# The channel loop of an attention and state-space training step: shared strips for the lag products, parameters for two blocks at once, basis rows in 2 KB pieces, states laid out by step

## The chip, the cores and the metric

The kernel runs on one core of a Trainium2 chip. The metric is the time of one execution on the device in microseconds (us), as the median of several runs; the time before is 2,733.29 us (three runs, 2,728.04 to 2,741.99). The profile is that of one further execution.

## The reference

A forward pass and all its gradients. The input x (2,048 tokens by 576 channels) goes through 32-head attention (`a`) and through a state-space convolution (`b`), and a gate mixes the two. The part that the change touches is `b` and its gradient:

```
logdA = dt * A                                   # A, B, C: 576 channels x 128 states, complex
P = exp(logdA[:, :, None] * l[None, None, :])    # l = 0 .. 2047
K = einsum("dn,dnl,dn->dl", C, P, dt * B).real   # one kernel of 2048 taps per channel
y = causal convolution of x with K, per channel (by FFT), + u * Dskip
out = g * a + (1 - g) * y
```

Returned are `out` and the gradients with respect to x, the attention's weights, A, B, C, log_dt, Dskip and the gate's weights. The kernel does the convolution without an FFT, in 16 time blocks of 128 tokens: within a block by a 128 x 128 Toeplitz matrix made of the first 128 taps, across blocks by 128 complex states per channel that step from block to block.

## The kernel before

There are three long stages: projections and attention with its gradients (to about 2,050 us), the channel loop (about 2,137 to 2,565 us, with a run-up before it), and a closing stage with the output projections. The order of the instructions on each engine is written out by hand; each engine, and SP and POOL as queues that issue transfers, takes its own in that order.

Beside attention, POOL computes the basis: for each channel the powers of its state factors, 128 states by real and imaginary part by 128 offsets, and stores it in DRAM as `E_d`, four channels (2 KB per partition) at a time (line 555).

The channel loop (lines 1481 to 1565) runs over 18 blocks of 32 channels. Iteration i finishes block i, steps the states of i+1, and prepares i+2 (`sb`) and i+3 (`mb`). What matters here, in the order of an iteration:

- `scan_open` and `scan` (704 to 733): DVE steps the states `HG` of blocks i and i+1 through 15 time blocks, two chains taken alternately, three instructions per step and chain. The factors come from `par`. `HG` has its four parts (real and imaginary, forward and backward in time) outermost and the step next.
- `rw1`, `rw2` (744 to 755): DVE weights the states with `par` and packs them as `Rw` for PE.
- `m_sum`, `m_fin` (637 to 648): PE sums the sheared lag products `skw` of block i+2 into the gradient of the first 128 taps.
- `m_part` (611 to 622), twice for block i+3, 16 channels each: for a channel one matmul of 128 x 32 weights (`gyp`: 16 columns of the incoming gradient, 16 of zeros) with 128 columns of `xs`, into its own 32 rows of a PSUM tile. The lower 16 rows get zeros. ACT copies the tile to `mst`; SP stores it in DRAM as `Md_d`, 32 rows of 144 floats per channel.
- `m_load` (604): POOL loads the next `xs` (1 MB, 8 KB per partition) and `gyp`. `m_skw` (629): SP reads `Md_d` back with a row pitch one element shorter than the rows, which turns diagonals into columns; the 16 columns of zeros that end each row of `mst` fill the corners.
- `sums` (847) and `load_par` (668) on POOL; `turn_e` (655): PE transposes the basis `E1n` of block i+2 and ACT copies it out as `E1e`; `k0` and `k0_out` (761, 772): PE makes the first 128 taps of block i+1, ACT copies them, SP stores them in `Kp_d`.
- `uv` (688): PE projects x and the gradient onto the basis, ACT copies to `UV`. `t0` (778): PE applies the Toeplitz matrix `T0w`; `t0_load` (853): SP loads the next `T0w` from `Kp_d` with overlapping rows (1 MB, 8 KB per partition), one buffer.
- `ybp` (787): PE adds what the states give (`Rw` with `E1n`), and when a half of `E1n` is used up, `load_en` (678) has POOL load half of block i+3 into its place (1 MB, 8 KB per partition).
- `yd_out`, `pairs1`, `pairs2`, `psum` (797 to 839): results out, and products of the two state chains, which PE sums.

So SP's order in an iteration is: two stores of `Md_d`, four sheared loads `skw`, the store of `Kp_d`, the load of `T0w`. POOL's is: `xs`, `gyp`, two additions, three loads of `par`, the two halves of `E1n`, and in turn `RXn` or `yd_d`. In the run-up (1447 to 1480, and 1270 to 1279 beside the end of attention) SP issues all loads.

Of the kernel before, what the change touches and what calls it, by code (L numbers as in the profile page):

```python
# [17 lines left out]
P = 128  # L18


def build(tc, aps, dbg_aps=None, stages=("s1", "attn", "post", "s4", "final")):
# [40 lines left out]
    with ExitStack() as gctx:  # L62
# [33 lines left out]
        E_d = dram.tile([P, D, 2, P], BF, name="E_d")  # L96
# [7 lines left out]
        Md_d = dram.tile([D, 2 * SUB, MW], F32, name="Md_d")  # L104
# [382 lines left out]
        def basis_ops(pool, k0, k1):  # L487
# [41 lines left out]
            def e_main(k, c):  # L529

                q = k * CE + c
                nl = (NA - 1) * NBT

                def first():
                    Eo[q] = pool.tile([P, EH, 2, P], BF, tag="Eo", bufs=2, name="Eo")
                    pl(Eo[q][:, :, :, 0:NBT], T_[:, :, c:c + EH, 0:NBT].rearrange("p r c b -> p c r b"),
                       sgn.unsqueeze(1).unsqueeze(3).to_broadcast([P, EH, 2, NBT]), A.mult)
                eops.append((0.45, first))
                for ri in range(2):
                    st = []  # L540
# [63 lines left out]
        def m_load(b, dma=nc.gpsimd.dma_start):  # L604
            xs = xss[b] = Q["pl"].tile([P, NSUB, SUB, CB], BF, tag="xs", bufs=1, name="xs")
            src = bass.AP(tensor=xb_d.tensor, offset=xb_d[b:b + 1, 0:1, 0:1].offset,
                          ap=[[XR * SUB * CB, NB], [SUB * CB, NSUB], [1, NSUB * SUB * CB]])
            dma(xs.rearrange("p e t c -> p (e t c)"), src)
            dma(Q["gyp2"][b % 2][:, 0:SUB, :].rearrange("p t c -> p (t c)"), gyb_d[b])

        def m_part(b, u):
            d0 = b * CB
            gyp, xs = Q["gyp2"][b % 2], xss[b]
# [8 lines left out]
            Q["mdma"](Md_d[d0 + u * 16:d0 + (u + 1) * 16].rearrange("(q g) t w -> (g t) q w", g=4), mst)  # L622
# [6 lines left out]
        def m_skw(b):  # L629
            skw = skws[b] = Q["pl"].tile([P, CB // 8, P], F32, tag="skw", name="skw")  # L630
            for v in range(CB // 8):
                dd = b * CB + v * 8
                src = bass.AP(tensor=Md_d.tensor, offset=Md_d[dd:dd + 1, 0:1, SUB - 1:SUB].offset,
                              ap=[[2 * SUB * MW, 8], [MW - 1, SUB], [1, P]])
                Q["mdma"](skw[:, v, :], src)
# [31 lines left out]

        def load_par(b, dma=nc.gpsimd.dma_start):
            if b == NBLK - 1:
                par = Q["pw"].tile([P, XB, NCOL], BF, tag="RX", bufs=2, name="par_l").bitcast(F32)[:, 0:12, :]  # L670
            else:
# [32 lines left out]
        def scan_open(b):  # L704
            B_ = blk(b)
            HG = B_["HG"] = Q["pw"].tile([P, 4, NS, CB], F32, tag="HG", bufs=2, name="HG")
            UVk = B_["UVk"] = B_["UV"][:, :, 0:2 * NB, :].rearrange("p r (s k) c -> p r s k c", s=2)
            nc.vector.tensor_copy(HG[:, :, 0, :].rearrange("p (r s) c -> p r s c", s=2), UVk[:, :, :, 0, :])

        def scan(*chains):  # L710

            def part(b, s_):
                B_ = blk(b)
                HG, ZZ = B_["HG"], B_["par"][:, 0:8, :].rearrange("p (m q) c -> p m q c", m=2)
                if s_ is None:
                    return HG, ZZ, B_["UVk"], 4
                return HG[:, s_::2], ZZ[:, :, s_::2], B_["UVk"][:, :, s_:s_ + 1], 2

# [3 lines left out]
            for t in range(max(k1 - k0 for _, _, k0, k1 in todo_)):  # L722
                live = [(x, p_, k0 + t) for x, p_, k0, k1 in todo_ if k0 + t < k1]
                tz = {}
                for x, (HG, ZZ, UVk, n), k in live:
                    tz[x] = Q["pw"].tile([P, 2, 4, CB], F32, tag=f"tz{x}", bufs=2, name="tz")[:, :, 0:n]
                    nc.vector.tensor_tensor(tz[x], HG[:, :, k - 1, :].unsqueeze(1).to_broadcast([P, 2, n, CB]), ZZ, op=A.mult)
                for x, (HG, ZZ, UVk, n), k in live:
                    t0v = tz[x][:, 0].rearrange("p (r s) c -> p r s c", r=2)
                    nc.vector.tensor_tensor(t0v, t0v, UVk[:, :, :, k, :], op=A.add)  # L730
                for x, (HG, ZZ, UVk, n), k in live:
                    t0v, t1v = [tz[x][:, m].rearrange("p (r s) c -> p r s c", r=2) for m in range(2)]
                    nc.vector.tensor_tensor(HG[:, :, k, :].rearrange("p (r s) c -> p r s c", r=2), t0v, t1v[:, ::-1], op=A.add)

        def cast1(b, nm, s_):
            B_ = blk(b)
            HGv = B_["HG"].rearrange("p (r s) k c -> p r s k c", s=2)
            B_[nm] = Q["pw"].tile([P, 2, NS, CB], BF, tag=nm, name=nm)
            nc.scalar.copy(B_[nm], HGv[:, :, s_, ::-1, :])
# [4 lines left out]
        def rw1(b):  # L744
            B_ = blk(b)
            for nm, r_, tg in (("wa", 8, "wA"), ("wb", 9, "wB")):
                B_[nm] = Q["pw"].tile([P, 4 * NS, CB], F32, tag=tg, name=nm)
                nc.vector.tensor_tensor(B_[nm], B_["HG"].rearrange("p q k c -> p (q k) c"),  # L748
                                        B_["par"][:, r_, :].unsqueeze(1).to_broadcast([P, 4 * NS, CB]), op=A.mult)
# [7 lines left out]
        def wk_cast(b):  # L757
            wk = blk(b)["wk"] = Q["pw"].tile([P, 2, CB], BF, tag="wk", bufs=2, name="wk")
            nc.scalar.copy(wk, blk(b)["par"][:, 10:12, :])
# [101 lines left out]
        def open_loads():  # L861
# [3 lines left out]
            Q["gyp2"], Q["mst2"] = [], []  # L865
# [4 lines left out]
            for u in range(2):  # L870
                m_u = Q["pl"].tile([P, 4, MW], F32, tag=f"mst{u}", name=f"mst{u}")
                nc.gpsimd.memset(m_u[:, :, P:MW], 0.0)
                Q["mst2"].append(m_u)
# [20 lines left out]
        def load_xtok():  # L894
            x_v = x2.rearrange("(t p) d -> p t d", p=P)
            for nm, shape, dt_, n in (("xs", [P, NSUB, SUB, CB], BF, 7), ("RXn", [P, 2 * NB, XB], BF, 3), ("gyp0", [P, 2 * SUB, CB], BF, 1),
                                      ("gyp1", [P, 2 * SUB, CB], BF, 1), ("mst0", [P, 4, MW], F32, 2), ("mst1", [P, 4, MW], F32, 2)):
# [49 lines left out]
        if "attn" in stages:  # L947
# [5 lines left out]
            with ExitStack() as ctx:  # L953
# [316 lines left out]
                for x, f in ((15, lambda: pt_close("a", open_loads)), (15, lambda: m_load(0, nc.sync.dma_start)), (17, lambda: load_rx(0, nc.sync.dma_start)),  # L1270
                             (21, lambda: m_part(0, 0)), (22, lambda: m_part(0, 1)), (23, lambda: pt_close("b", lambda: open_en(0))),
# [138 lines left out]
        if "s4" in stages:  # L1410
# [8 lines left out]
            with ExitStack() as ctx:  # L1419
# [27 lines left out]
                with tc.manual_schedule(engines={mybir.EngineType.SP}):  # L1447
# [13 lines left out]
                    m_part(1, 0)  # L1461
                    m_part(1, 1)
# [11 lines left out]
                    m_part(2, 0)  # L1474
                    m_part(2, 1)
# [5 lines left out]
                    for i in range(NBLK):  # L1481
# [38 lines left out]
                        if sb == NBLK - 1:  # L1520
                            load_par(sb)
# [303 lines left out]
```

## Time and profile before

| | |
|---|---|
| median of three runs | 2,733.29 us |
| the profiled execution | 2,736.89 us |
| its span, first to last instruction | 2,734.8 us |
| PE busy | 2,414.4 us (88%) |
| ACT busy | 2,356.0 us (86%) |
| DVE busy | 2,301.4 us (84%) |
| POOL busy | 1,803.1 us (66%) |
| mean granted clock of PE | 0.962 |
| moved by DMA | 492.20 MB in 1,169,461 packets |

The busy times are averages over stages of different kinds: in the attention stage ACT is busy all the time, in the channel loop PE, DVE and the DMA engines are all near full, and in the closing stage PE is. A row of the profile names the line, the engine, the operation and its tiles; "SPq" and "POOL ... DMA_DIRECT2D" are issues of transfers, whose own time is only that of the issue. Idle time stands in brackets with the work that ended it. Some transfers of the loop, with the median time from issue to landing, which the profile gives for those that POOL issues:

| transfer | count, size | us to landing |
|---|---|---|
| `E1n` from `E_d` (POOL) | 30 of 1,024 KB | 6.6 |
| `xs` from `xb_d` (POOL) | 14 of 1,024 KB | 12.1 |
| `par` from `par_d` (POOL) | 45 of 64 KB | 7.6 |
| `T0w` from `Kp_d` (SP) | 18 of 1,024 KB | not given |
| `Md_d` from `mst` (SP) | 36 of 288 KB | not given |
| `skw` from `Md_d` (SP) | 72 of 64 KB | not given |

### The profile page before, as it was taken

The numbers are of one execution on the slowest core, as the hardware profiler recorded it, in microseconds if no ns is written. First come the engines' busy times: TensorE is split into PE (matmuls) and PEld (weight loads), VectorE is DVE, ScalarE is ACT, GpSimd is POOL, SyncE is SP. The second block draws the span as 40 slices with busy tenths as digits, with TensorE's granted clock in tenths as the row PEclk, the third lists the DMA queues.
The fourth block names the chain that finished last, engine by engine and source line by source line (L and its number), as shares of the span: only waits on it lengthen the run. The fifth ranks groups of instructions, "written<-read, shape, count | busy, mean of one in ns | idle before, by whom it ended". The sixth has DMA issues, their size and how long they took to land. (4 is left out here: it accounts for less than half of the span.)

```text
span 2734.8 us, 70124 instructions
## 1 busy us (share of the span) xinstructions
PE 2414.4 (88%) x27411; PEld 1148.3 (42%) x27411; DVE 2301.4 (84%) x4142; ACT 2356.0 (86%) x2744; POOL 1803.1 (66%) x2856
## 2 busy tenths in 40 slices
PE   8798989999888988988998898998986789898889
PEld 4433333333333333333333333333323688888656
DVE  4749999999899999999999999998975798889864
ACT  5489999999999999999999999999974789788211
POOL 0179888888888888798888878888601244335321
PEclk9989999999999999999999999999977899999989
DMA  7637799879879978977988898797779799887894
GB/s 226 186 97 164 149 170 177 159 163 178 169 154 175 177 151 169 185 155 163 171 167 158 160 179 161 157 177 153 147 134 223 195 251 249 235 251 236 236 266 126
DMA packets 1169461, 492.20 MB, mean 180 GB/s; under 512 B 1074341, under 2 KB 1132310, under 8 KB 1160426
## 3 DMA queue, kind: packets, MB, share of 16 engines
q1 hardware_dynamic: 1128234, 346.80, 64.5%
q0 software_dynamic: 38880, 135.43, 18.4%
q10 hardware_dynamic: 2016, 5.51, 0.6%
q8 instruction: 214, 3.51, 0.6%
q14 instruction: 117, 0.96, 0.1%
HBM read 147.12 MB, written 98.52 MB: 90 GB/s over the span
## 5 line engine op out<-in xcount | busy, mean ns | idle before, releaser
L1389 DVE TENSOR_TENSOR ds<-ps_P,PT 128x512 bf16<-128x512 f32 x2048 | 1312.4, 683 | 125.1 <-PE ps_P L30 86.3
L1384 ACT ACTIVATE eb<-ps_P 128x1024 bf16<-128x1024 f32 x1024 | 1097.7, 1072 | 36.5 <-PE ps_P L30 36.5
L1379 ACT ACTIVATE PT<-ps_P 128x1024 bf16<-128x1024 f32 x1024 | 1101.9, 1077 | 20.7 <-PE ps_P L30 19.6
L30 PE MATMUL ps_P<-dOaT,VaT_g 32*128 32x512 bf16 x2048 | 580.5, 387 | 31.4 <-DVE ds L1389 16.1
L502 POOL TENSOR_TENSOR et<-eG,eT 128x448 f32<-128x448 f32 x576 | 543.0, 963 | 10.7
L30 PE MATMUL ps_P<-QaT_g,KaT_g 32*128 32x512 bf16 x2048 | 401.2, 384 | 139.2 <-ACT PT L1379 124.6
L30 PE MATMUL ps_P<-KaT_g,QaT_g 32*128 32x512 bf16 x2048 | 405.3, 388 | 1.9 <-ACT eb L1384 1.4
L30 PEld LDWEIGHTS <-KaT_g 32*128 32x128 bf16 x2048 | 147.5, 91 | 467.3 <-issue 451.5
L502 POOL TENSOR_TENSOR Eo<-et,et 128x448 bf16<-128x448 f32 x288 | 327.3, 1136 | 20.7
L30 PEld LDWEIGHTS <-QaT_g 32*128 32x128 bf16 x2048 | 116.0, 91 | 284.5 <-issue 262.1
L30 PE MATMUL accV<-eb,dOa 128*32 128x512 bf16 x2048 | 185.0, 394 | 27.9 <-ACT eb L1384 27.9
L30 PE MATMUL accO<-PT,Vtok_g 128*32 128x512 bf16 x2048 | 206.2, 392 | 0.1
L30 PE MATMUL accK<-dsT,Qtok_g 128*32 128x256 bf16 x4096 | 162.7, 280 | 16.5 <-DMA dsT<-ds 14.6
L30 PE MATMUL accQ<-ds,Ktok_g 128*32 128x512 bf16 x2048 | 159.9, 390 | 2.3 <-DVE dvacc L1146 2.2
L30 PEld LDWEIGHTS <-Vtok_g 128*32 128x32 bf16 x2048 | 52.7, 93 | 222.1 <-issue 222.1
L666 ACT COPY E1e<-etp 128x1024 bf16<-128x1024 bf16 x132 | 125.1, 1045 | 22.3 <-PE etp L665 22.2
L1097 DVE COPY dsT<-turn_p 128x1024 bf16<-128x1024 bf16 (+1 forms) x216 | 139.1, 644 | 2.1 <-PE turn_p L1092 2.1
L1092 PE MATMUL turn_p<-ident_bf,ds 128*128 128x128 bf16 x1664 | 134.5, 223 | 1.5 <-DVE gb L1164 0.8
L502 POOL TENSOR_TENSOR et<-eT 128x32 f32<-128x32 f32 (+3 forms) x288 | 116.2, 423 | 11.4
L30 PEld LDWEIGHTS <-Qtok_g 128*32 128x32 bf16 x4096 | 87.7, 97 | 81.4 <-issue 57.8
L1092 PEld LDWEIGHTS <-ds 128*128 128x128 bf16 x1664 | 97.6, 99 | 49.1 <-issue 49.1
L555 POOL DMA_DIRECT2D E_d<-Eo x144 | 85.0, 590 | 42.8 <-POOL Eo L502 42.8
(296 smaller groups left out, 3715.0 us busy)
## 6 DMA issues: line engine op xcount, KB each, us to landing
E_d<-Eo POOLq DMA_DIRECT2D x144, 256.0 KB, 3.3
E1n<-E_d POOLq DMA_DIRECT2D x30, 1024.0 KB, 6.6
T0w<-Kp_d SPq DMA_DIRECT2D x18, 1024.0 KB
xs<-xb_d POOLq DMA_DIRECT2D x14, 1024.0 KB, 12.1
Md_d<-mst SPq DMA_DIRECT2D x36, 288.0 KB
dsT<-ds SPq DMA_TRANSPOSE x512
dqkv_d<-dtk POOLq DMA_DIRECT2D x96, 72.0 KB, 4.2
skw<-Md_d SPq DMA_DIRECT2D x72, 64.0 KB
```

What stands on the lines that cost most here:

```text
L30: return nc.tensor.matmul(out, lhsT=lhsT, rhs=rhs, start=start, stop=stop, **kw)
L502: nc.gpsimd.tensor_tensor(out, a, b, op=op)
L555: nc.gpsimd.dma_start(E_d[:, q:q + EH], Eo.pop(q))
L666: copy(E_[:, 4 * q:4 * q + 4], pt_)
L1092: nc.tensor.transpose(pt_[:, x, qb, :], t_[:, qb * P:(qb + 1) * P], ident_bf)
L1097: (nc.scalar.copy if NTOT <= now[0] < NTOT + OFF else nc.vector.tensor_copy)(o_(), pt_[:, x:x + n])
L1379: nc.scalar.activation(U["PT"][i, j // 2], ps, ACT.Exp)
L1384: nc.scalar.activation(e, ps, ACT.Exp)
L1389: nc.vector.tensor_tensor(U["ds"][i][:, j, :], ps, U["PT"][i, j // 2][:, j % 2, :], op=A.mult)
```

## The change

Five edits go together.

1. `m_part` runs once per block. Two channels share a 32-row strip: `gyp` gets zeros on both sides of its 16 columns, the first channel's weights are taken so that its columns are the upper 16, the second's so that they are the lower 16, and the second matmul adds to the first. One PSUM tile, one copy and one store then hold the block; `Md_d` is laid out as `mst` is, so a partition's 2,304 B go out in one piece. `m_skw` reads it with the new pitch.
2. `load_par` loads eight rows of parameters for two blocks in one transfer (before, twelve rows, four of them twice, for one block in three transfers); a view `par_of` picks a block. It is called in odd iterations only, and the special case of the last block goes.
3. `E_d` gets a gap of 32 B after every four channels, so that a row of the basis is read in pieces of 2 KB, not 8 KB.
4. `xs` is loaded in two halves.
5. `HG` and `Rw` have the step outside the two time directions; the factors are repeated over the directions by a broadcast view.

The tiles that hold x for the last gradients are fitted to the new sizes (`load_xtok`). The core of the diff:

```
-        E_d = dram.tile([P, D, 2, P], BF, name="E_d")
+        EQ = 4
+        E_d = dram.tile([P, D // EQ, EQ * 2 * P + 16], BF, name="E_d")
...
-        Md_d = dram.tile([D, 2 * SUB, MW], F32, name="Md_d")
+        Md_d = dram.tile([NBLK, P, 4, MW], F32, name="Md_d")
...
-                            nc.gpsimd.dma_start(E_d[:, q:q + EH], Eo.pop(q))
+                            nc.gpsimd.dma_start(E_d[:, q // EQ, 0:EQ * 2 * P], Eo.pop(q).rearrange("p c r n -> p (c r n)"))
...
         def m_load(b, dma=nc.gpsimd.dma_start):
...
-            dma(xs.rearrange("p e t c -> p (e t c)"), src)
-            dma(Q["gyp2"][b % 2][:, 0:SUB, :].rearrange("p t c -> p (t c)"), gyb_d[b])
+            n = NSUB // 2
+            for y in range(2):
+                src = bass.AP(tensor=xb_d.tensor, offset=xb_d[b:b + 1, y * n:y * n + 1, 0:1].offset,
+                              ap=[[XR * SUB * CB, NB], [SUB * CB, NSUB], [1, n * SUB * CB]])
+                dma(xs[:, y * n:(y + 1) * n].rearrange("p e t c -> p (e t c)"), src)
+            dma(Q["gyp2"][b % 2][:, SUB:2 * SUB, :].rearrange("p t c -> p (t c)"), gyb_d[b])
...
-        def m_part(b, u):
+        def m_part(b):
...
             for q in range(4):
                 for g_ in range(4):
-                    dd = u * 16 + 4 * q + g_
-                    mm(psM[32 * g_:32 * (g_ + 1), q, :].rearrange("p (a b) -> p a b", b=SUB), lhsT=gyp[:, :, dd],
-                       rhs=xs[:, ::-1, ::-1, dd], tile_position=(0, 32 * g_))
-            mst = Q["mst2"][u]
+                    for u in range(2):
+                        dd = 8 * q + 2 * g_ + u
+                        mm(psM[32 * g_:32 * (g_ + 1), q, :].rearrange("p (e t) -> p e t", t=SUB), lhsT=gyp[:, (1 - u) * SUB:(3 - u) * SUB, dd],
+                           rhs=xs[:, ::-1, ::-1, dd], start=(u == 0), stop=(u == 1), tile_position=(0, 32 * g_))
+            mst = Q["mst"]
             nc.scalar.copy(mst[:, :, 0:P], psM)
-            Q["mdma"](Md_d[d0 + u * 16:d0 + (u + 1) * 16].rearrange("(q g) t w -> (g t) q w", g=4), mst)
+            Q["mdma"](Md_d[b], mst)
...
-                              ap=[[2 * SUB * MW, 8], [MW - 1, SUB], [1, P]])
-                Q["mdma"](skw[:, v, :], src)
+                              ap=[[SUB * 4 * MW, NSUB], [4 * MW - 1, SUB], [1, P]])
+                Q["mdma"](skw[:, q, :], src)
...
-                par = Q["pl"].tile([P, 12, CB], F32, tag="par", bufs=3, name="par")
-            blk(b)["par"] = par
-            for s_ in range(2):
-                dma(par[:, s_:8:2, :], par_d[:, 0:4, b * CB:(b + 1) * CB])
-            dma(par[:, 8:12, :], par_d[:, 4:8, b * CB:(b + 1) * CB])
+            par = pars_[b] = Q["pl"].tile([P, 8, XB], F32, tag="par", bufs=2, name="par")
+            dma(par, par_d[:, 0:8, b * XB:(b + 1) * XB])
+
+        def par_of(b):
+            return pars_[b // 2][:, :, b % 2 * CB:(b % 2 + 1) * CB]
...
-                dma(En[:, x * n:(x + 1) * n], E_d[:, dG + x * n:dG + (x + 1) * n])
+                dma(En[:, x * n:(x + 1) * n].rearrange("p (g c) r n -> p g (c r n)", c=EQ),
+                    E_d[:, (dG + x * n) // EQ:(dG + (x + 1) * n) // EQ, 0:EQ * 2 * P])
...
-            HG = B_["HG"] = Q["pw"].tile([P, 4, NS, CB], F32, tag="HG", bufs=2, name="HG")
+            HG = B_["HG"] = Q["pw"].tile([P, 2, NS, 2, CB], F32, tag="HG", bufs=2, name="HG")
...
-                    nc.vector.tensor_tensor(tz[x], HG[:, :, k - 1, :].unsqueeze(1).to_broadcast([P, 2, n, CB]), ZZ, op=A.mult)
+                    nc.vector.tensor_tensor(tz[x], HG[:, :, k - 1].unsqueeze(1).to_broadcast([P, 2, 2, n, CB]),
+                                            ZZ.unsqueeze(3).to_broadcast([P, 2, 2, n, CB]), op=A.mult)
...
-            Rw, En = B_["Rw"].rearrange("p r (s k) c -> p r s k c", s=2), B_["En"].pop(h)
+            Rw, En = B_["Rw"].rearrange("p r (k s) c -> p r s k c", s=2), B_["En"].pop(h)
...
-                g_u = Q["pl"].tile([P, 2 * SUB, CB], BF, tag=f"gyp{u}", name=f"gyp{u}")
-                nc.gpsimd.memset(g_u[:, SUB:2 * SUB, :], 0.0)
+                g_u = Q["pl"].tile([P, 3 * SUB, CB], BF, tag=f"gyp{u}", name=f"gyp{u}")
+                for y in (0, 2):
+                    nc.gpsimd.memset(g_u[:, y * SUB:(y + 1) * SUB, :], 0.0)
...
-                            if sb + 1 < NBLK:
-                                load_par(sb)
+                            if i % 2 == 1 and (i + 3) // 2 < NBLK // 2:
+                                load_par((i + 3) // 2)
...
-                        if sb == NBLK - 1:
-                            load_par(sb)
```

In the compiled order of the changed kernel, POOL issues per block two loads of `xs` instead of one, and one load of `par` per two blocks; SP issues one store of `Md_d` instead of two. PE has the same number of instructions, ACT 18 copies fewer, and DVE the same scan instructions with other strides.

More of the change, by code (lines that the diff above doesn't have):

```diff
@@ L605, in m_load @@
             xs = xss[b] = Q["pl"].tile([P, NSUB, SUB, CB], BF, tag="xs", bufs=1, name="xs")
-            src = bass.AP(tensor=xb_d.tensor, offset=xb_d[b:b + 1, 0:1, 0:1].offset,
-                          ap=[[XR * SUB * CB, NB], [SUB * CB, NSUB], [1, NSUB * SUB * CB]])
-            dma(xs.rearrange("p e t c -> p (e t c)"), src)
-            dma(Q["gyp2"][b % 2][:, 0:SUB, :].rearrange("p t c -> p (t c)"), gyb_d[b])
-        def m_part(b, u):
-            d0 = b * CB
-            gyp, xs = Q["gyp2"][b % 2], xss[b]
+            n = NSUB // 2
[5 more added lines that the diff above has]
+        def m_part(b):
+            gyp = Q["gyp2"][b % 2]
+            xs = xss[b]
             psM = Q["psM"]()
@@ L629, in m_skw @@
         def m_skw(b):
[L630 to L633, printed above, removed]
-                              ap=[[2 * SUB * MW, 8], [MW - 1, SUB], [1, P]])
-                Q["mdma"](skw[:, v, :], src)
+            skw = skws[b] = Q["pl"].tile([P, 4, P], F32, tag="skw", name="skw")
+            for q in range(4):
+                src = bass.AP(tensor=Md_d.tensor, offset=Md_d[b:b + 1, 0:1, q:q + 1, SUB - 1:SUB].offset,
+                              ap=[[SUB * 4 * MW, NSUB], [4 * MW - 1, SUB], [1, P]])
+                Q["mdma"](skw[:, q, :], src)
         def m_sum(b):
@@ L666, in turn_e @@
                 copy(E_[:, 4 * q:4 * q + 4], pt_)
+        pars_ = {}
         def load_par(b, dma=nc.gpsimd.dma_start):
-            if b == NBLK - 1:
-                par = Q["pw"].tile([P, XB, NCOL], BF, tag="RX", bufs=2, name="par_l").bitcast(F32)[:, 0:12, :]
-            else:
-                par = Q["pl"].tile([P, 12, CB], F32, tag="par", bufs=3, name="par")
-            blk(b)["par"] = par
-            for s_ in range(2):
-                dma(par[:, s_:8:2, :], par_d[:, 0:4, b * CB:(b + 1) * CB])
-            dma(par[:, 8:12, :], par_d[:, 4:8, b * CB:(b + 1) * CB])
+            par = pars_[b] = Q["pl"].tile([P, 8, XB], F32, tag="par", bufs=2, name="par")
+            dma(par, par_d[:, 0:8, b * XB:(b + 1) * XB])
+        def par_of(b):
+            return pars_[b // 2][:, :, b % 2 * CB:(b % 2 + 1) * CB]
         def load_en(b, h, dma=nc.gpsimd.dma_start, pieces=1):
@@ L705, in scan_open @@
             B_ = blk(b)
-            HG = B_["HG"] = Q["pw"].tile([P, 4, NS, CB], F32, tag="HG", bufs=2, name="HG")
+            HG = B_["HG"] = Q["pw"].tile([P, 2, NS, 2, CB], F32, tag="HG", bufs=2, name="HG")
             UVk = B_["UVk"] = B_["UV"][:, :, 0:2 * NB, :].rearrange("p r (s k) c -> p r s k c", s=2)
-            nc.vector.tensor_copy(HG[:, :, 0, :].rearrange("p (r s) c -> p r s c", s=2), UVk[:, :, :, 0, :])
+            nc.vector.tensor_copy(HG[:, :, 0], UVk[:, :, :, 0, :])
         def scan(*chains):
@@ L713, in part @@
                 B_ = blk(b)
-                HG, ZZ = B_["HG"], B_["par"][:, 0:8, :].rearrange("p (m q) c -> p m q c", m=2)
+                HG, ZZ, UVk = B_["HG"], par_of(b)[:, 0:4].rearrange("p (m r) c -> p m r c", r=2), B_["UVk"]
                 if s_ is None:
-                    return HG, ZZ, B_["UVk"], 4
-                return HG[:, s_::2], ZZ[:, :, s_::2], B_["UVk"][:, :, s_:s_ + 1], 2
+                    return HG, ZZ, UVk, 2
+                return HG[:, :, :, s_:s_ + 1], ZZ, UVk[:, :, s_:s_ + 1], 1
             todo_ = []
@@ L725, in scan @@
                 for x, (HG, ZZ, UVk, n), k in live:
-                    tz[x] = Q["pw"].tile([P, 2, 4, CB], F32, tag=f"tz{x}", bufs=2, name="tz")[:, :, 0:n]
-                    nc.vector.tensor_tensor(tz[x], HG[:, :, k - 1, :].unsqueeze(1).to_broadcast([P, 2, n, CB]), ZZ, op=A.mult)
+                    tz[x] = Q["pw"].tile([P, 2, 2, 2, CB], F32, tag=f"tz{x}", bufs=2, name="tz")[:, :, :, 0:n]
+                    nc.vector.tensor_tensor(tz[x], HG[:, :, k - 1].unsqueeze(1).to_broadcast([P, 2, 2, n, CB]),
+                                            ZZ.unsqueeze(3).to_broadcast([P, 2, 2, n, CB]), op=A.mult)
                 for x, (HG, ZZ, UVk, n), k in live:
-                    t0v = tz[x][:, 0].rearrange("p (r s) c -> p r s c", r=2)
-                    nc.vector.tensor_tensor(t0v, t0v, UVk[:, :, :, k, :], op=A.add)
+                    nc.vector.tensor_tensor(tz[x][:, 0], tz[x][:, 0], UVk[:, :, :, k, :], op=A.add)
                 for x, (HG, ZZ, UVk, n), k in live:
-                    t0v, t1v = [tz[x][:, m].rearrange("p (r s) c -> p r s c", r=2) for m in range(2)]
-                    nc.vector.tensor_tensor(HG[:, :, k, :].rearrange("p (r s) c -> p r s c", r=2), t0v, t1v[:, ::-1], op=A.add)
+                    nc.vector.tensor_tensor(HG[:, :, k], tz[x][:, 0], tz[x][:, 1, ::-1], op=A.add)
         def cast1(b, nm, s_):
             B_ = blk(b)
-            HGv = B_["HG"].rearrange("p (r s) k c -> p r s k c", s=2)
             B_[nm] = Q["pw"].tile([P, 2, NS, CB], BF, tag=nm, name=nm)
-            nc.scalar.copy(B_[nm], HGv[:, :, s_, ::-1, :])
+            nc.scalar.copy(B_[nm], B_["HG"][:, :, ::-1, s_, :])
         def rw2_open(b):
@@ L745, in rw1 @@
             B_ = blk(b)
-            for nm, r_, tg in (("wa", 8, "wA"), ("wb", 9, "wB")):
+            for nm, r_, tg in (("wa", 4, "wA"), ("wb", 5, "wB")):
                 B_[nm] = Q["pw"].tile([P, 4 * NS, CB], F32, tag=tg, name=nm)
-                nc.vector.tensor_tensor(B_[nm], B_["HG"].rearrange("p q k c -> p (q k) c"),
-                                        B_["par"][:, r_, :].unsqueeze(1).to_broadcast([P, 4 * NS, CB]), op=A.mult)
+                nc.vector.tensor_tensor(B_[nm], B_["HG"].rearrange("p r k s c -> p (r k s) c"),
+                                        par_of(b)[:, r_, :].unsqueeze(1).to_broadcast([P, 4 * NS, CB]), op=A.mult)
         def rw2(b):
@@ L758, in wk_cast @@
             wk = blk(b)["wk"] = Q["pw"].tile([P, 2, CB], BF, tag="wk", bufs=2, name="wk")
-            nc.scalar.copy(wk, blk(b)["par"][:, 10:12, :])
+            nc.scalar.copy(wk, par_of(b)[:, 6:8, :])
         def k0(b):
@@ L864, in open_loads @@
             Q["pl"] = cm.__enter__()
-            Q["gyp2"], Q["mst2"] = [], []
+            Q["gyp2"] = []
             for u in range(2):
-                g_u = Q["pl"].tile([P, 2 * SUB, CB], BF, tag=f"gyp{u}", name=f"gyp{u}")
-                nc.gpsimd.memset(g_u[:, SUB:2 * SUB, :], 0.0)
+                g_u = Q["pl"].tile([P, 3 * SUB, CB], BF, tag=f"gyp{u}", name=f"gyp{u}")
+                for y in (0, 2):
+                    nc.gpsimd.memset(g_u[:, y * SUB:(y + 1) * SUB, :], 0.0)
                 Q["gyp2"].append(g_u)
[L870 to L873, printed above, removed]
+            Q["mst"] = Q["pl"].tile([P, 4, MW], F32, tag="mst", name="mst")
+            nc.gpsimd.memset(Q["mst"][:, :, P:MW], 0.0)
             rights.append(cm)
@@ L895, in load_xtok @@
             x_v = x2.rearrange("(t p) d -> p t d", p=P)
-            for nm, shape, dt_, n in (("xs", [P, NSUB, SUB, CB], BF, 7), ("RXn", [P, 2 * NB, XB], BF, 3), ("gyp0", [P, 2 * SUB, CB], BF, 1),
-                                      ("gyp1", [P, 2 * SUB, CB], BF, 1), ("mst0", [P, 4, MW], F32, 2), ("mst1", [P, 4, MW], F32, 2)):
+            for nm, shape, dt_, n in (("xs", [P, NSUB, SUB, CB], BF, 7), ("RXn", [P, 2 * NB, XB], BF, 3), ("gyp0", [P, 3 * SUB, CB], BF, 2),
+                                      ("gyp1", [P, 3 * SUB, CB], BF, 2), ("mst", [P, 4, MW], F32, 2)):
                 t_ = Q["pl"].tile(shape, dt_, tag=nm, bufs=1, name="x_" + nm)
@@ L1270, in build @@
                 for x, f in ((15, lambda: pt_close("a", open_loads)), (15, lambda: m_load(0, nc.sync.dma_start)), (17, lambda: load_rx(0, nc.sync.dma_start)),
-                             (21, lambda: m_part(0, 0)), (22, lambda: m_part(0, 1)), (23, lambda: pt_close("b", lambda: open_en(0))),
+                             (21, lambda: m_part(0)), (23, lambda: pt_close("b", lambda: open_en(0))),
                              (25, lambda: m_skw(0)), (31, lambda: pt_close("c", lambda: open_en(1))),
@@ L1460, in build @@
                     turn_e(0, 1, 0, 4, dve_copy)
-                    m_part(1, 0)
-                    m_part(1, 1)
+                    m_part(1)
                     m_skw(1)
@@ L1473, in build @@
                     uv(1, 0)
-                    m_part(2, 0)
-                    m_part(2, 1)
+                    m_part(2)
                     m_skw(2)
@@ L1496, in build @@
                         if mb is not None:
-                            m_part(mb, 0)
-                            m_part(mb, 1)
+                            m_part(mb)
                             if mb + 1 < NBLK:
```

## The prediction

> **What bounds the kernel now.** First the table of stretches: until about 2,050 us the attention stage keeps ACT full (500.00 of 500 us in the stretch from 1,000 to 1,500), and the change leaves its instructions alone but for where its basis stores land. The channel loop, from about 2,137 to 2,565 us, is where all edits lie. So I listed the start of each block's state scan there (DVE, line 708):
>
> ```profile
> 2285.67 0.23 DVE L708 CAST HG<-UV 128x128 f32<-128x128 bf16 x1
> 2307.51 0.23 DVE L708 CAST HG<-UV 128x128 f32<-128x128 bf16 x1
> 2338.16 0.23 DVE L708 CAST HG<-UV 128x128 f32<-128x128 bf16 x1 [8.26 <-ACT UV L702]
> ```
>
> Columns: start, length, what ran, idle before it with its releaser. One block takes 21.84 us, the next 30.65. The sixteen distances from 2,137.34 to 2,526.57 are 29.8, 22.3, 21.85, 23.2, 29.25, 21.85, 21.85, 30.65, 21.85, 21.85, 27.6, 24.5, 22.6, 25.8, 21.85, 22.4: 389.2 us. The table of stretches, cut at these points, tells floor from excess:
>
> ```profile
> 2286.00:2307.50 21.50, 20.57 (x386) 19.36 (x384) 21.36 (x51) 20.16 (x33) 10.71 (x10) 1.00 0.98 270
> 2307.50:2338.00 30.50, 22.55 (x390) 21.18 (x387) 21.81 (x53) 20.53 (x33) 10.49 (x11) 0.89 0.80 216
> ```
>
> Columns: length, busy PE, weight loads, DVE, ACT, POOL, then granted clock, DMA share, GB/s. DVE's work is the same 21.4 to 21.8 us in both: **the floor of a block is DVE**, and 389.2 - 16 x 21.85 = 39.6 us is excess. In a long block PE stands still for a transfer, and DVE waits for what PE then hands over through ACT:
>
> ```profile
> 2328.61 2.10 PE L30 MATMUL yp<-RX,T0w 128*128 128x32 bf16 x32 [7.11 <-DMA T0w<-Kp_d]
> ```
>
> Why T0w is late stands in SP's timeline; SP issues every step of this in order:
>
> ```profile
> 2292.57 1.26 SPq L622 DMA_DIRECT2D Md_d<-mst  x2
> 2304.76 4.02 SPq L635 DMA_DIRECT2D skw<-Md_d  x4
> 2308.82 0.46 SPq L776 DMA_DIRECT2D Kp_d<-K0c  x1
> 2316.62 0.34 SPq L859 DMA_DIRECT2D T0w<-Kp_d  x1
> 2317.01 3.19 SPq L622 DMA_DIRECT2D Md_d<-mst  x2
> ```
>
> The sheared loads (635) stand from 2,293.8 to 2,304.8 for the landing of the lag stores; K0c was ready at 2,297.2 on ACT, but its store (776) is behind them; T0w (859) then waits for that store. The cycle from one store of Md to the next is 24.4 us here, over DVE's 21.85: SP falls behind until PE has to wait. Over the loop SP's waits are:
>
> ```profile
> SPq L635 <- DMA Md_d<-mst: 160.9, 24, 14.3
> SPq L859 <- DMA Kp_d<-K0c: 77.5, 17, 8.0
> ```
>
> (us, times, longest). So the end is set by **SP's chain of landings**, not by bandwidth alone.
>
> **The change, part by part.**
>
> *Lag products and their store.* Per block, two stores of 512 rows of 576 B become one of 128 rows of 2,304 B: 576 KB become 288, and 16 engines get 8 rows each instead of 64. The trace has no such store. Bounds for its landing: below, 2.9 us, what the present stores took at 2,134.42 and 2,148.95, when the first sheared load went out 2.9 us after them; above, today's 12 us, if the landing is only the queue ahead (T0w went out 2.2 us before Md at 2,290.35, in the same hardware queue). I take 4 to 5: what is short of the rows is gone, some contention stays. Then, from a block's start: the copy of mst ends at +7.7 us (the second one of today; the first half now waits for all 32 matmuls), landing +12.5, four sheared loads of 0.59 us to +15, Kp_d's store +15.5, its landing 4.6 (77.5/17) to +20, T0w landing in 7.7 (2,290.35 to its use at 2,298.06) to 12 (2,316.62 to 2,328.61): +28 to +32. PE asks at +12.4 of the next block, +34.2. Cover 2 to 6 us, and SP is free 9 us before the next Md. The waits for T0w (33.0 us, 9 times) and for skw in the loop go. ACT loses one copy of 0.59 us a block; in a floor block it isn't the last, so nothing. If the new cover is gone, up to 31.7 us return.
>
> *PE.* Still 32 matmuls, but now two in a row add into the same strip. Lower bound 0. Upper bound: each second waits out the first's 419 ns, 16 x 0.42 = 6.7 us a block. Nearest rows: the sums misc<-pq, which also add into one place, run 59 in 3.47 us, 59 ns each; psM today 32 in 2.09 us, 65 ns. I take 0; up to 0.86 us a block hides in PE's wait for Rw (0.86 <- DVE Rw in the floor blocks).
>
> *Basis in 2 KB pieces.* E1n (2 MB a block) comes as 512 pieces per load, not 128 rows of 8 KB. POOL's issue grows from 549 to about 760 ns (today's par loads, 512 pieces each, take 757 to 767): hidden, POOL waits 2.9 and 4.2 us before each. Here the Trainium skill speaks against the change: DMA: Bandwidth & Descriptors, "How a descriptor splits into AXI transactions", says that a piece which does not begin at a multiple of 256 B also fetches the bytes before it. The new pitch is 2,080 B, so pieces begin 0 to 224 B past such a point, 3.5 of 64 beats on average: an estimate of 5.5% on E1n, 2.1 MB / 270 GB/s = 7.8 us, so +0.43 us of DMA time a block. The row: from 2,600 to 2,620 us the load of go_all, in rows of 1,152 B that are no multiple of 256 either, moves 350 to 394 GB/s, more than the loop's 270 with 8 KB rows. By the row it is 0. Against it stand 0.28 MB of Md and 0.06 MB of parameters less, 0.34 MB / 270 GB/s = 1.3 us. The DMA share of a floor block, 0.98 x 21.5 = 21.1 us, becomes 19.8 (row) or 20.2 (rule); I take the row's, and either lies under 21.85. Stores of the basis in the attention stage (144, landing 3.3 us) have some 12 us per pair of buffers: hidden.
>
> *Parameters.* Three loads of 512 rows of 128 B per block become one of 1,024 of 256 B per two blocks; POOL loses about 2.3 us of issue a block, which nothing waits for. A new wait: in odd blocks the load reuses the tile that rw1 of this block reads until 2,300.8, and POOL comes there at 2,298.7. Behind it is load_en, which waits for PE until 2,305.2 anyway: 0. If that cover went, 2 us at every second block. Moved too: the last block's special load, 0.4 us.
>
> *xs in halves:* one issue more (0.55 us) on POOL; lands 12.1 us after issue, used 20.8 us after (2,293.07 to 2,313.83): 0.
>
> *States by step:* the same elements in the same number of DVE instructions (tz 419 ns for 128x256, 286 for the others); only strides differ. 0; bounds +-0.1 us per block on the floor.
>
> *Before the loop* SP loses an Md issue and four par issues (3 us) and gains 0.6; PE's waits for skw, 4.07 and 3.22 us, and the wait for gyp to 2,147.05 behind the same SP queue shrink. DMA stays over its share of 1.0 there: I take 4 of a possible 10 us.
>
> **Sum.** Without the first distance (8 us of excess, start-up) the loop holds 31.7 us. I take 25: some meetings of transfers stay. With 4 before the loop: 29 us. Behind the loop the chain goes from the last yp through yd_d's landing to SP's loads, so the end moves along. The profiled execution, 2,736.9 us (span 2,734.8 and 2.1 around), would be 2,708; the median shown is 3.6 lower, so 2,704, rounded to **2,705 us** (-1.0%).
>
> **Rivals.**
> 1. *E1n becomes the late transfer* (0.14). Its first half goes out at +19.6 and is used at +28.9: 9.3 us, and it lands in 6.6 (8.6 at most). T0w would now be sent at about the same moment with 8 KB rows against pieces of 2 KB. If E1n then needs 11.3 us, 2.0 - 0.86 = 1.1 us x 16 = 18 us are given back: gain 11, 2,722 us. Against: T0w and E1n together are 2.1 MB, 7.8 us at 270 GB/s.
> 2. *Landings don't fall* (0.12), since T0w's rows ahead in the queue, not Md's own, make the 12 us. Then only lighter DMA work helps, about a third: gain 10, 2,723 us. For it: 0.98 of share in floor blocks. Against: 2.9 us when nothing was ahead.
> 3. *Slower* (0.12): one mechanism, E1n in pieces. If it lands as slowly as xs of the same size does (12.1 us) and somewhat more, every block's turn_e stops PE. It decides from 9.3 + 0.86 + 29/16 = 12.0 us on; at 13 us the loss is 2.8 x 16 = 45, less 29: +16, 2,749 us. For it: xs's 12.1. Against: the go_all row.
> 4. *The strips serialize* or an edit does less than it says: the program has one store of 128x576 a block and the same PE count, so it does what it says; the strip is excluded as far as the two PE rows reach.
>
> **Numbers.** Forecast 0.62, rivals 0.14, 0.12 and 0.12. Less than 0.5% (14 us) can't be told from no change here. Rivals 1 and 2 lie near that edge, a third of them beyond it: faster 0.62 x 0.95 + 0.08 = 0.67; slower 0.13; same 0.20. The forecast's own range is 2,692 (all 39.6 us and a little) to 2,719; with rivals 1 and 2 it reaches 2,731.
>
> **What would show it.** Right: starts of line 708 some 22 us apart nearly throughout; SP's wait for Md under 60 us; no wait for T0w; tz still 419 ns; psM 32 in at most 2.9 us. Wrong: PE's etp waiting for E1n, E1n landing beyond 10 us, or SP's wait for Md above 120.

## The result, and the profile after

The changed kernel takes 2,702.76 us (median of 6 runs, 2,694.2 to 2,712.26), beside 2,735.97 us for the kernel before (6 runs, 2,728.04 to 2,743.97): 33 us less, ratio 0.9864 with a 95% interval of 0.984 to 0.9889. The forecast was 2,705 us.

The profiled execution after took 2,694.2 us, the shortest of its six and 42.7 less than that of before. The starts of the state scans split this. Timeline of DVE, changed kernel (start, length, what ran, idle before it and its releaser); the scan is now line 711:

```profile
2126.34 0.23 DVE L711 CAST HG<-UV 128x128 f32<-128x128 bf16 x1 [10.57 <-ACT UV L705]
2153.46 0.23 DVE L711 CAST HG<-UV 128x128 f32<-128x128 bf16 x1 [3.40 <-ACT UV L705]
2175.30 0.23 DVE L711 CAST HG<-UV 128x128 f32<-128x128 bf16 x1
...
2284.81 0.23 DVE L711 CAST HG<-UV 128x128 f32<-128x128 bf16 x1
2306.65 0.23 DVE L711 CAST HG<-UV 128x128 f32<-128x128 bf16 x1
2330.00 0.23 DVE L711 CAST HG<-UV 128x128 f32<-128x128 bf16 x1 [1.48 <-ACT UV L705]
...
2484.08 0.23 DVE L711 CAST HG<-UV 128x128 f32<-128x128 bf16 x1 [1.11 <-ACT UV L705]
```

The same sixteen distances, from 2,126.34 to 2,484.08, are 357.7 us, 31.5 less than the 389.2 of before. From the last of these starts to the end it is 208.2 us in both kernels (2,692.3 - 2,484.1 and 2,734.8 - 2,526.6). The other 11 us lie before 2,126.34, and the runs don't show them to be the change's: other variants of the changed kernel, with the same attention stage, begin this stretch at 2,139.6, 2,142.0 and 2,148.8 us. So what lies before the loop scatters by some 20 us between executions. Below, kernels are therefore compared by their sixteen distances as well as by their medians.

Twelve of the sixteen distances are now within 0.05 us of DVE's floor of 21.85 us. The table of stretches (length, busy PE, weight loads, DVE, ACT, POOL, granted clock, DMA share, GB/s) for two of them and the one from 2,306.5:

```profile
2263.00:2285.00 22.00, 21.14 (x396) 19.89 (x394) 21.86 (x54) 20.04 (x32) 8.56 (x8) 1.00 0.85 250
2285.00:2306.50 21.50, 20.61 (x386) 19.37 (x384) 21.36 (x52) 19.48 (x32) 10.43 (x10) 1.00 0.92 263
2306.50:2330.00 23.50, 22.56 (x392) 21.34 (x390) 21.88 (x53) 20.34 (x33) 8.88 (x8) 0.93 0.89 258
```

DVE is busy all through a floor block, and the DMA engines, at 0.98 of a floor block before, have some air. PE is close behind DVE: 21.1 of 22.0 us. In the third stretch it is the longer one. The granted clock there is 0.93 instead of 1.00 and PE needs 22.6 us, though it waits for no transfer; DVE then waits 1.48 us for what PE hands over.

PE's waits for transfers in the loop show what the change took away. Before, from 2,160 to 2,530 us (engine, tile and line, what it waited for: total us, times, longest):

```profile
PEld L30 <- DMA T0w<-Kp_d: 17.0, 5, 7.3
PE yp L30 <- DMA T0w<-Kp_d: 16.0, 4, 7.1
PE misc L30 <- DMA skw<-Md_d: 9.2, 8, 3.4
```

The first two rows are the same four stalls, seen once on PE's weight loads and once on its matmuls, and so are not added: PE stood still 16.0 us for T0w and 9.2 us for skw. In the changed kernel both are gone from this stretch. Its matmuls with T0w (count, busy us, mean ns, and last the idle time before them, which was 16.1 us):

```profile
L30 PE MATMUL yp<-RX,T0w 128*128 128x32 bf16 x512 | 33.5, 225 | 0.0
```

SP's timeline shows how one block's chain now fits, though less shortened than forecast:

```profile
2270.84 0.32 SPq L626 DMA_DIRECT2D Md_d<-mst  x1
2277.85 2.47 SPq L638 DMA_DIRECT2D skw<-Md_d  x4
2280.36 0.46 SPq L777 DMA_DIRECT2D Kp_d<-K0c  x1
2283.60 0.33 SPq L860 DMA_DIRECT2D T0w<-Kp_d  x1
2292.93 0.32 SPq L626 DMA_DIRECT2D Md_d<-mst  x1
2301.74 2.47 SPq L638 DMA_DIRECT2D skw<-Md_d  x4
```

From the lag store to the first sheared load it is 7.0 and 8.8 us, not 12. T0w goes out at 2,283.60, and SP then stands idle for 9.0 us until the next lag store, where before it was already late. SP's waits in the loop (waiting line, what for: total us, times, longest) turn round accordingly; it waits most for ACT's copy, that is, for the next block's work:

```profile
SPq L626 <- ACT mst L625: 124.9, 16, 11.6
SPq L638 <- DMA Md_d<-mst: 109.6, 17, 8.9
SPq L860 <- DMA Kp_d<-K0c: 56.3, 17, 6.4
```

### The profile page after: what moved, and what is told of

It is laid out like the page before. It is cut to its first block, busy times and chain, and to the rows that moved or that the text cites. A ratio compares the mean times of both kernels' runs of the same rounds, so it can differ in the third digit from the quotient of the medians.

```text
span 2692.3 us, 70041 instructions
## 1 busy us (share of the span) xinstructions
PE 2404.9 (89%) x27411; PEld 1138.0 (42%) x27411; DVE 2300.6 (85%) x4142; ACT 2343.5 (87%) x2726; POOL 1786.8 (66%) x2829
## 4 chain that ended last, share of the span: by engine, by line
ACT 39%; PE 25%; DVE 24%; issue 6%; DMA 3%; POOL 2%; SPq 1%; ACTq 0%; DVEq 0%; POOLq 0%
ACT eb L1384 23%; ACT PT L1379 15%; DVE ds L1389 7%; PE ps_P L30 7%; DVE tz L730 3%; PE accV L30 2%; PE ps_dx L30 2%; PE turn_p L1092 2%; PE ps_proj L30 2%; DVE tz L733 2%; DVE HG L735 1%; DVE wa L749 1%; DVE wb L749 1%; DVE pq L810 1%; PE accK L30 1%
## 5 line engine op out<-in xcount | busy, mean ns | idle before, releaser
L1044 POOL TENSOR_TENSOR dOa<-dO_b,rl 128x288 bf16<-128x288 bf16 x32 | 21.5, 673 | 143.0 <-DVE rl L1039 142.9
```

## The experiments

Three theories stood at the start. A: SP's chain of landings sets the loop, and the lag store opens it. B: rows of 8 KB in POOL's queue hold the small transfers up, and the 2 KB pieces free them. C: DMA work as a whole. All measured values are in one table. "Md" and "Kp" are SP's waits for the landing of the lag store and of the taps' store, in us in all, from 2,085 to 2,560 us of each span. Each ratio is to runs of the kernel before that were taken together with that kernel.

| kernel | median us | ratio to before (95%) | sixteen distances | Md | Kp |
|---|---|---|---|---|---|
| before | | 1 | 389.2 | 160.9 | 83.8 |
| changed | 2,702.8 | 0.9864 (0.984 to 0.9889) | 357.7 | 109.6 | 61.3 |
| md_alone | 2,721.8 | 0.9931 (0.9905 to 0.9958) | 364.2 | 143.8 | 81.1 |
| skw_late_before | 2,769.7 | 1.0119 (1.0078 to 1.0161) | 418.7 | 4.9 | 103.8 |
| before_skw_prev | 2,721.3 | 0.9927 (0.9903 to 0.9952) | 370.6 | none | 127.3 |
| after_rows576 | 2,722.1 | 0.9921 (0.9895 to 0.9948) | 377.7 | 150.5 | 67.9 |
| after_8kb | 2,708.6 | 0.9887 (0.9852 to 0.9922) | 357.3 | 111.5 | 59.7 |
| pieces_alone | 2,739.5 | 0.9987 (0.9959 to 1.0015) | 381.8 | 163.4 | 90.9 |
| after_par_old | 2,709.1 | 0.9879 (0.9858 to 0.9901) | 356.8 | 120.0 | 64.3 |
| after_xs_whole | 2,718.3 | 0.9916 (0.9889 to 0.9943) | 364.5 | 150.9 | 77.4 |
| xs_halves_alone | 2,728.5 | 0.995 (0.9923 to 0.9976) | 374.5 | 139.5 | 101.2 |
| md_xs | 2,711.4 | 0.9895 (0.9849 to 0.9941) | 355.2 | 108.5 | 76.1 |
| after_xs_quarters | 2,713.4 | 0.9889 (0.9833 to 0.9944) | 359.4 | 99.4 | 61.5 |
| after_load_first | 2,708.6 | 0.9881 (0.9847 to 0.9915) | 357.5 | 108.1 | 67.9 |

The distances come from one profile each. Kernels at the floor agree within some 4 us (355.2 to 359.4); where blocks stall they scatter more. What these kernels keep over the floor, beside the first distance, lies nearly all in blocks with a granted clock under 0.95: 2.6 of 2.9 us in the changed kernel (two blocks), all of the 5.1 in after_xs_quarters (four blocks).

### The lag store alone: md_alone

The kernel before with part 1 only (strips, one copy, one store, the new shear). Of its edit, the store:

```
...
-            Q["mdma"](Md_d[d0 + u * 16:d0 + (u + 1) * 16].rearrange("(q g) t w -> (g t) q w", g=4), mst)
+            Q["mdma"](Md_d[b], mst)
...
```

> The kernel before with part 1 alone: shared strips, one copy and one store of 128 rows of 2,304 B per block, the new shear. Theory A (SP's chain of landings, opened by the lag store): most of the gain, 22 to 32 us (ratio 0.988 to 0.992), SP's wait for Md_d falls from 160.9 us to 100 to 120, and no or little waiting for T0w. Theory B (the 8 KB rows of the basis hold up the small transfers; pieces of 2 KB let them through): under 10 us, T0w still waited for some 20 us. Theory C (DMA work as a whole): this part has 0.28 of the 0.34 MB that go per block, so some 25 us, without telling it from A.

25.0 of the 31.5 us of the loop come with this part, and no wait for T0w or skw is left from 2,160 to 2,530 us. SP's wait fell to 143.8 us only, short of the 100 to 120 expected. The median's ratio, 0.9931, lies outside the range expected: 19 us, not 22 to 32, though the interval reaches into it.

What stays in this kernel is mostly not waiting for transfers. Of its 8.8 us over the floor in the fifteen distances after the first, 7.8 lie in six blocks whose granted clock is 0.93. One of them, and the block at the floor from 2,330.0 us (columns as in the table of stretches):

```profile
2283.65:2306.93 23.28, 22.35 (x390) 21.14 (x387) 21.72 (x53) 20.21 (x32) 10.65 (x10) 0.93 0.98 273
2329.98:2351.84 21.86, 21.00 (x392) 19.77 (x390) 21.72 (x53) 19.89 (x32) 10.52 (x10) 1.00 0.95 261
```

PE's 21.0 us become 22.35, past DVE's 21.72. What lowers the clock in some blocks and not in others, the runs do not show.

### Is it the chain? skw_late_before and before_skw_prev

The first moves the sheared loads behind T0w's load on SP:

```
                                 m_load(mb + 1)
-                            m_skw(mb)
...
                             t0_load(i + 1)
+                        if mb is not None:
+                            m_skw(mb)
```

> The kernel before with the same transfers, rows and bytes; only the four sheared loads of a block are issued behind the load of T0w instead of ahead of the store of Kp_d, so that T0w does not wait for the landing of Md_d. Theory A: 20 to 30 us faster (ratio 0.989 to 0.993), the waits for T0w (33 us) gone; skw may now be a little late. Theory C (DMA work) and theory B (row sizes): no change, ratio 0.998 to 1.002, since not one byte or row differs.

It became 26 us slower than before (2,769.7 beside 2,743.7), the opposite of what theory A had said. The wait for T0w did go, but PE now waited for skw. PE's and ACT's waits in the loop of this kernel:

```profile
PEld misc L30 <- DMA skw<-Md_d: 55.9, 31, 9.4
ACT RX L646 <- PE misc L30: 53.6, 12, 9.9
PE misc L30 <- DMA skw<-Md_d: 52.0, 28, 9.2
```

and SP's timeline shows why:

```profile
2280.23 0.38 SPq L622 DMA_DIRECT2D Md_d<-mst  x1
2284.03 0.33 SPq L776 DMA_DIRECT2D Kp_d<-K0c  x1
2292.42 0.33 SPq L859 DMA_DIRECT2D T0w<-Kp_d  x1
2292.94 2.77 SPq L635 DMA_DIRECT2D skw<-Md_d  x4
```

The taps' store, now directly behind the lag stores, takes 8.4 us until T0w may go, and skw stands behind T0w's 1 MB in the same queue. Both results of the chain, T0w and skw, are needed once a block. This reordering only changed which is late. Theory A in the form "T0w must not wait for Md_d" falls; the length of the whole chain remains.

The second test takes the wait away and leaves everything else in its place:

```
-                dd = b * CB + v * 8
+                dd = max(b - 1, 0) * CB + v * 8
```

> The kernel before, whose sheared loads of a block read the lag products of the block before it, so that the gradient of the first taps is that of the neighbouring block. Every transfer, row and byte is as before, and in the same order; only the wait for the landing of this block's two stores is gone from SP's chain. Theory A (SP's chain): the sixteen distances fall from 389 us to 355 to 362, the waits for T0w go, the time falls by 22 to 32 us (ratio 0.988 to 0.992). If it is the DMA work or the row count as such that holds the loop, nothing changes: 385 to 393 us, ratio above 0.997.

18.6 us of the sixteen distances went, with every row and byte still there, so theory C can't be the whole; the expected 27 to 34 were not reached. PE's wait for skw nearly went (0.9 us), but that for T0w only fell, from 16.0 us to:

```profile
PE yp L30 <- DMA T0w<-Kp_d: 9.9, 4, 4.3
```

SP's timeline tells where the rest stayed:

```profile
2289.50 1.36 SPq L622 DMA_DIRECT2D Md_d<-mst  x2
2291.04 6.79 SPq L635 DMA_DIRECT2D skw<-Md_d  x4
2297.87 1.78 SPq L776 DMA_DIRECT2D Kp_d<-K0c  x1
2306.62 0.34 SPq L859 DMA_DIRECT2D T0w<-Kp_d  x1
```

SP now waits 7 us on average and 8.8 here for Kp_d's 8 KB store to land, 127.3 us in all over the loop instead of 83.8. The likely reading is that the rows of Md_d, for which nobody waits any more, still lie ahead, and the next landing in SP's chain pays. That was not tested apart from the sheared loads, which go out right before that store too.

### Rows or bytes? after_rows576

The changed kernel with its one store cut into 512 rows of 576 B, the same 288 KB:

```
-        Md_d = dram.tile([NBLK, P, 4, MW], F32, name="Md_d")
+        Md_d = dram.tile([NBLK, 4, P, MW], F32, name="Md_d")
...
-            Q["mdma"](Md_d[b], mst)
+            Q["mdma"](Md_d[b].rearrange("q p w -> p q w"), mst)
...
```

The sheared loads read the new layout with the row pitch of the kernel before.

> The changed kernel, whose one store of 288 KB per block is cut into 512 rows of 576 B instead of 128 of 2,304 B (Md_d laid out by quarter, partition, column). It tells rows from bytes within part 1. If the number of rows makes the landing: SP's mean wait for Md_d of 6.4 us goes up to 8 to 10 us; the time stays within 8 us of the changed kernel, since the chain has some 7 us of cover. If the bytes or the queue ahead make it: 6.4 us stays within 0.7 us, and the time within 3 us.

SP's mean wait rose from 6.4 to 8.9 us (150.5/17), as expected if rows count. But the 7 us of cover did not hold: the sixteen distances rose by 20 us, and PE waited for T0w again. SP's waits in this kernel, and PE's:

```profile
SPq L638 <- DMA Md_d<-mst: 150.5, 17, 12.9
SPq L626 <- ACT mst L625: 93.8, 16, 11.5
PE yp L30 <- DMA T0w<-Kp_d: 11.1, 4, 3.8
```

Joining the rows is worth 14 to 20 us here. The 20 compare this kernel's slowest execution of nine, which is the profiled one, with the changed kernel's fastest; its median is 13.6 us above that of after_8kb, taken together with it, and the two ranges do not meet. The halved bytes can own at most the rest of the loop's 31.5 us.

### The other edits

The gap in E_d, taken out of the changed kernel, and put alone into the kernel before:

```
-        E_d = dram.tile([P, D // EQ, EQ * 2 * P + 16], BF, name="E_d")
+        E_d = dram.tile([P, D // EQ, EQ * 2 * P], BF, name="E_d")
```

> The changed kernel without the gap of 32 B in E_d, so that the basis is again read in rows of 8 KB. Theory A: as the changed kernel within 5 us (ratio to before 0.985 to 0.989). Theory B: most of the gain goes, ratio above 0.994, T0w late again. Were the pieces dear[...], this would be faster than the changed kernel by up to 6 us.

> The kernel before with the basis in pieces of 2 KB alone. E1n is sent 10 us and more after Md_d. If it were in the way of the lag store or of Kp_d's, the sixteen distances fall below 383 us. As the changed kernel lost nothing without the pieces: 385 to 393 us, ratio 0.997 to 1.003.

Neither does anything that can be measured: 357.3 us without the pieces, and alone a ratio of 0.9987 (0.9959 to 1.0015), which leaves room for 11 us at most. Alone, its distances were 381.8 us, 3 below the range I had given, in a kernel that still stalls. Theory B is not borne out for the basis.

The parameters, in the main:

```
-            par = pars_[b] = Q["pl"].tile([P, 8, XB], F32, tag="par", bufs=2, name="par")
-            dma(par, par_d[:, 0:8, b * XB:(b + 1) * XB])
+            par = pars_[b] = Q["pl"].tile([P, 12, CB], F32, tag="par", bufs=3, name="par")
+            for s_ in range(2):
+                dma(par[:, s_:8:2, :], par_d[:, 0:4, b * CB:(b + 1) * CB])
+            dma(par[:, 8:12, :], par_d[:, 4:8, b * CB:(b + 1) * CB])
...
```

> The changed kernel with the parameters loaded as before: three loads of 512 rows of 128 B for every block. Part 1 alone left the sixteen distances at 364.2 us, the whole change at 357.7; 6.5 us are without an owner. If it is the parameters (short rows in the way of Md_d): 362 to 366 us, SP's mean wait for Md_d up from 6.4 to some 8 us. If they do nothing: 356 to 359 us. In the time at most 8 us, ratio 0.985 to 0.991.

Nothing in the loop: 356.8 us.

xs in one piece, in the changed kernel, and halves alone in the kernel before. The first:

```
-            n = NSUB // 2
-            for y in range(2):
-                src = bass.AP(tensor=xb_d.tensor, offset=xb_d[b:b + 1, y * n:y * n + 1, 0:1].offset,
-                              ap=[[XR * SUB * CB, NB], [SUB * CB, NSUB], [1, n * SUB * CB]])
+            src = bass.AP(tensor=xb_d.tensor, offset=xb_d[b:b + 1, 0:1, 0:1].offset,
+                          ap=[[XR * SUB * CB, NB], [SUB * CB, NSUB], [1, NSUB * SUB * CB]])
...
```

> The changed kernel with xs loaded in one piece of 1 MB with rows of 8 KB. If the halves own the 6.5 us: the sixteen distances 362 to 366 us and SP's mean wait for Md_d near 8 us; xs is issued at nearly the same moment as Md_d, and its rows are the largest in the way. If not: 356 to 359 us, ratio 0.984 to 0.989.

> The kernel before with xs in halves alone. Theory: rows of the hardware queue and of POOL's queue are served in turn on each engine, and Md_d with 64 rows per engine meets xs, which is sent at the same moment; with rows of 4 KB each turn is shorter. SP's wait for Md_d falls from 160.9 to 110 to 140 us and the sixteen distances from 389 to 372 to 383 us. If only the row count of Md_d matters: 386 to 392.

Halves alone take the kernel before from 389.2 to 374.5 us, ratio 0.995 (0.9923 to 0.9976). xs goes out on POOL within 1 us of the lag store (2,292.26 and 2,292.93 in the changed kernel). So theory B holds for another transfer than the one it was thought of.

Beside part 1 the halves are worth some 7 to 13 us: 364.5 us with whole rows beside 357.7, and medians 9.2 us (after_xs_whole beside after_par_old) and 13.3 us (md_alone beside after_8kb) higher. Each pair was taken together, and its ranges do not meet; the parameters, and in the second pair the states' layout, differ too, but with part 1 and the halves alone the loop is no longer (md_xs). Against the changed kernel itself the intervals of after_xs_whole just touch. How the halves act there is shown only in part. With whole rows PE waits again, 3.2 us for T0w and 3.1 for skw (2,175 to 2,505 us):

```profile
PE yp L30 <- DMA T0w<-Kp_d: 3.2, 3, 1.8
PE misc L30 <- DMA skw<-Md_d: 3.1, 6, 0.9
```

But in md_alone, which has whole rows too, PE waits for neither, and the blocks of low clock hold the excess. That both kernels stand at 364 us is chance in part.

With rows of 2 KB (four loads, n = NSUB // 4):

> The changed kernel with xs in four loads with rows of 2 KB. SP's mean wait for Md_d is 8.9 us with rows of 8 KB and 6.4 with 4 KB. If turns between rows set it: 4.8 to 5.8 us. If the 1 MB as such does: 6.0 to 6.8. The sixteen distances hardly move, 354 to 358 us, since DVE's floor is 349.6 and the first distance holds 5.3 of the rest; POOL issues 1.1 us more per block, which is covered.

SP's waits, first with 8 KB rows of xs, then with 2 KB:

```profile
SPq L636 <- DMA Md_d<-mst: 150.9, 17, 11.6
```

```profile
SPq L638 <- DMA Md_d<-mst: 99.4, 17, 8.0
```

With 8, 4 and 2 KB the mean wait is 8.9, 6.4 and 5.8 us: it falls with the row size at the same 1 MB. (Other kernels with the joined store have 8.5 with 8 KB, and 6.4 to 7.1 with 4 KB; 2 KB stands in one run.) Time is no longer won, since DVE's floor holds; the distances, 359.4 us, came out 1.4 over the range given, with four blocks at a granted clock of 0.93.

Both edits that count, without the three that don't:

> The kernel before with two of the five edits, part 1 (strips and one store) and xs in halves. Undone singly in the changed kernel, neither the parameters nor the pieces of the basis moved the sixteen distances (356.8 and 357.3 against 357.7 us), xs did (364.5). If these two edits are all that counts: 356 to 360 us, SP's mean wait for Md_d 6 to 7.5 us, ratio to before 0.985 to 0.990. If the other three matter together: above 362.

355.2 us and a ratio of 0.9895 (0.9849 to 0.9941). These two are enough for the loop's whole gain. The medians of md_xs and the changed kernel overlap in their intervals, so neither is shown to be the faster.

### A try to go further: after_load_first

In the run-up the loads of xs go ahead of the sheared loads:

```
-                    m_skw(1)
                     m_load(2, nc.sync.dma_start)
+                    m_skw(1)
...
+                    m_load(3, nc.sync.dma_start)
                     m_skw(2)
                     uv(1, 1)
-                    m_load(3, nc.sync.dma_start)
```

> The changed kernel, in whose run-up SP issues the loads of xs and gyp of blocks 2 and 3 ahead of the sheared loads of blocks 1 and 2, in the time in which it waits for Md_d to land. PE waits 4.7 us for gyp at 2,136 us, and the first distance is 27.1 us, 5.3 over the floor. If that wait is what makes the first distance long: 22 to 24 us, PE's wait for gyp gone, 3 to 5 us faster than the changed kernel in the loop. If the stores of Md_d then land later behind 1 MB of xs, skw is late instead and nothing is won.

PE's wait for gyp went, and the first distance fell from 27.1 to 25.5 us, but skw came up to 8.0 us late instead; the sixteen distances are the same, 357.5 us. It isn't faster than the changed kernel. No run showed a version that beats it.

## Why the prediction was right

*The bound was read rightly.* SP's cycle of landings was longer than DVE's block, and once it is shorter the blocks stand at DVE's floor: of the 31.7 us of excess in the fifteen distances after the first, 25 were taken and 28.8 measured (359.4 before, 330.6 after); the first distance gave another 2.7. I had kept 6.7 us for meetings of transfers; no wait of PE for a transfer remained, and of the 2.9 us that stay, 2.6 lie in two blocks at a granted clock of 0.93, a term that the sum did not have.

*One reading was wrong without touching the sum.* The 33.0 us of waits for T0w count PE's weight loads and its matmuls at the same stalls; PE stood still 16.0 us, and 9.2 more for skw. The forecast was taken from the distances, not from these waits.

*The term of the sum that was mis-sized is the landing of the lag store.* I took 4 to 5 us, by the present stores' 2.9 with nothing ahead; the waits behind the store's issue average 6.4 us, up to 8.9. The sign "SP's wait for Md under 60 us" did not come: it was 109.6. What made up for it: Kp_d's store landed in 3.3 us (56.3/17, from 2,137 us on), not 4.6, and T0w's arrival had enough cover left to cause no wait at all. The rows joined were the right lever; what else is in the way, xs above all, I had left out.

*xs in halves was set to 0 and is worth some 7 to 13 us* beside part 1, and 14.7 us of the distances alone. I had asked when xs itself is needed (20.8 us after its issue) and not whom it delays.

*The basis in pieces was set to 0, and is.* POOL's issue rose to 762 ns, as taken from the par loads; E1n lands in 6.5 us (6.6 before) and no PE wait for it showed. So the +0.43 us of DMA time a block that the prediction estimated from the Trainium skill (DMA: Bandwidth & Descriptors, "How a descriptor splits into AXI transactions") can't be seen in the time: the DMA share of a floor block lies under 1 in any case (0.85 and 0.92 in the two above). Whether the extra bytes are fetched no run tells.

*Strips, parameters, states.* psM's 32 matmuls take 2.08 to 2.19 us where they took 2.08 to 2.22: two sums into the same strip show no cost. The new wait of POOL for rw1 is there, 16.2 us in 7 times, 2.3 each beside the forecast 2, and nothing waits behind it. tz takes 418 ns (419 before), the two others of a step 284 each (286 before).

*The run-up* was given 4 us; the first distance fell by 2.7, and the step before it not at all (17.2 and 17.5 us). PE's waits for skw and gyp there stayed: they hang on the order of the loads.

*The rivals.* E1n late: no. Landings that don't fall: half true; SP's wait for them fell by a third (160.9 to 109.6 us), but that was enough. Slower by E1n: no. The forecast's -29 us against the measured -33 is closer than its parts deserve, and in that it was lucky: the landing was taken some 2 us too short, xs was left out, and the residue in the loop was 4 us too large.

## What to carry to other kernels

Where one queue issues a cycle of dependent transfers (store, load back, store, load), compare the length of the whole cycle, landings included, with the block time of the busiest engine. If it is longer, a wait on the other end of the kernel is only the symptom, and reordering may only move it elsewhere, as it did here. Shorten the landings: join the rows of the store that opens the chain, and cut the rows of the large transfer that is sent in the same microsecond. And cost a transfer by whom it delays, not only by when its own data are needed. Where two engines are nearly as long as a block, look at the granted clock before an edit is credited with the last few us.

## What the runs showed of the hardware

- The row count of a store bears on how long it takes to land beside other traffic: 288 KB in 512 rows of 576 B were waited for 8.9 us on average, in 128 rows of 2,304 B 6.4 us.
- The row size of another queue's transfer does so too: 8.9, 6.4 and 5.8 us beside 1 MB of xs in rows of 8, 4 and 2 KB. The rows of the two queues mix: in the changed kernel's records of single packets, over fourteen lag stores, the first row starts 1.7 to 4.4 us after the issue and the last ends 5.0 to 8.7 us after it, and 27 to 259 large rows of POOL's queue start in between. That fits rows of the two queues taking turns; the records do not name the DMA engine, so the turns themselves are not shown.
- Large rows on another transfer, E1n, sent some 11 us later, made no difference (357.3 against 357.7 us).
- In before_skw_prev, a store of 8 KB issued soon after 576 KB of short rows made SP wait 127.3 us in 18 blocks for its landing, against 61.3 in the changed kernel.
- A block in which PE has 21.0 us of work at a granted clock of 1.00 took 22.9 to 23.5 us, not 21.85, when the clock was 0.93 and no transfer was waited for to speak of (23.28 us in md_alone, 23.49 in after_load_first).
